# Attention and two MLPs on one core: the second and third weight blocks decoded through the staging buffer of the last attention pair

## The chip, the core and the metric

The kernel runs on one core of a Trainium2 chip. The core has a matrix engine (PE, with its weight loads shown as PEld), a vector engine (DVE), an activation engine (ACT), a general engine (POOL) and a queue engine (SP) that issues the transfers (DMA). Each engine works through its own queue strictly in order, so an instruction that waits holds up everything behind it on that engine. Engines wait for each other through semaphores. The metric is device time in microseconds of the whole program, one launch.

## The reference

```python
# q, k, v: (2, 8, 768, 64); centroids: (8, 16, 64)
q_assign, k_assign = argmax over 16 centroids of normalised q, k
mask = q_assign[:, :, :, None] == k_assign[:, :, None, :]
attn = softmax(where(mask, q @ k.T / 8, -1e9))
x = (attn @ v) as (1536, 512)            # token x (head, dim)
h = x @ w_in;   x = maximum(0.01 * h, h) @ w_out      # 512 -> 2048 -> 512
h = x @ w_in2;  out = (maximum(h, 0) ** 2) @ w_out2
```

All of it is float32. On the matrix engine each float32 factor is split into a high part and a low remainder, and a product is three matmuls (high·high, low·high, high·low).

## The kernel before

**Attention.** Heads are worked in 8 pairs of 6 units; a unit is 256 query rows of one head, and there are 48 (numbered 0 to 47, the last pair is 42 to 47). For each of a unit's two 128-row tiles PE makes the scores S (line 350), DVE takes the negated row maximum nm (373) and ACT the exponential e with its row sum r (383). ACT adds a small constant to r (394), DVE takes the reciprocal (397), POOL multiplies e by it (400). PE transposes e in three groups of four 128x128 blocks into T (413); of each, ACT writes the high part eh (424) and DVE the remainder el (430). PE multiplies both by V into A (448). There is one A buffer, so the next unit's A can start only when the two halves of this one are folded into xt, first by ACT (461), then by DVE (470). When a pair is done POOL splits xt into xh and xl (162 as `pool_copy`, 478); these are the first MLP's input.

**MLP.** The 1536 tokens are three blocks of 512, the hidden width 16 weight blocks of 128 for each MLP. A unit of the MLP is one weight block on one token block: 12 matmuls `h <- xh, xl x wh, wl` (725), t and g on ACT and DVE (738, 739), gh and gl (745, 746), and two units later 12 matmuls into o (767). The first token block needs no row of the last pairs, the other two need the last pair's xh and xl. There are four h buffers in PSUM and two of g.

**Weight blocks.** A block arrives as 1 MB of raw 64-bit numbers, wraw (121), and is decoded in six steps: load; mag on ACT (128, wt from wraw); shift, low and sign on DVE (132, 138, 145, all into wt); split, that is wh on ACT (156) and wl on POOL (157). Raw buffer and wt are single in each staging pool: a load waits until sign of the block before it has read wraw, and mag waits until wl of the block before it has read wt. `stg[0]` is opened at the last pair in memory that the pairs' preparation has left; `stg[1]` (`stgb`) is opened behind attention in memory that attention's tiles occupy, so its first load waits for the last transposes of the last unit. `EARLY` blocks are spread over the six units of the last pair; the others over the MLP's units by `plan`.

**Order.** PE, DVE, ACT and POOL follow an order written out by hand (`PLAN`) up to unit 42. From there a scheduler of the compiler sets the order on these engines, from its own estimate of times; so a change of what is decoded when changes the order of everything from the last pair on.

Of the kernel before, what the change touches and what calls it, by code (L numbers as in the profile page):

```python
# [8 lines left out]
F32 = mybir.dt.float32  # L9
F32R = mybir.dt.float32r  # L10
I32 = mybir.dt.int32
# [41 lines left out]
def attention_moe_moe_kernel(  # L53
# [14 lines left out]
    NT, DM = out.shape  # L68
# [3 lines left out]
    NU = NP * 2 * (KC // 2)  # L72
# [3 lines left out]
    NBLK = NT // N  # L76
    G = 4
    GROUPS = ([2, 2] + [G] * (NF // G - 1), [G] * (NF // G))
    EARLY = 2
    RING = 8  # L80
    WARM = (9,4,10)

# [29 lines left out]
    stg = []  # L112

    def decode_pieces(ci):

        m, f = divmod(ci, NF)
        st = {}

        def load():
            st["raw"] = stg[-1].tile([128, 2 * DM, 2], I32, tag="wraw", name="wraw")  # L120
            nc.sync.dma_start(
                out=st["raw"].rearrange("p a b -> p (a b)"), in_=(w1, w2)[m][f].bitcast(I32)
            )

        def mag():
            t = stg[-1].tile([128, 2 * DM], I32, tag="wt", name="wt")
            st["t"] = t
            nc.scalar.mul(out=t.bitcast(F32), in_=st["raw"][:, :, 1].bitcast(F32), mul=W_SHIFT)

        def shift():  # L130
            t = st["t"]
            nc.vector.tensor_scalar(
                out=t, in0=t, scalar1=3, scalar2=None, op0=ALU.logical_shift_left
            )

        def low():
            t = st["t"]
            nc.vector.scalar_tensor_tensor(  # L138
                out=t, in0=st["raw"][:, :, 0], scalar=29, in1=t,
                op0=ALU.logical_shift_right, op1=ALU.bitwise_or,  # L140
            )

        def sign():
            t = st["t"]
            nc.vector.scalar_tensor_tensor(
                out=t, in0=st["raw"][:, :, 1], scalar=-0x80000000, in1=t,
                op0=ALU.bitwise_and, op1=ALU.bitwise_or,
            )

        def split():  # L150
            t = st["t"].bitcast(F32)
            pool = next(q for q, n in ring if ci % RING < n)
            wh = pool.tile([128, 2 * DM], F32R, tag="wh", name="wh")
            wl = pool.tile([128, 2 * DM], F32R, tag="wl", name="wl")
            weights[m, f] = (wh, wl)
            nc.scalar.copy(out=wh, in_=t)  # L156
            nc.gpsimd.tensor_tensor(out=wl, in0=t, in1=wh.bitcast(F32), op=ALU.subtract)  # L157

        return [load, mag, shift, low, sign, split]

    def pool_copy(out, in_):
        nc.gpsimd.tensor_scalar(
            out=out, in0=in_, scalar1=1.0, scalar2=1.0, op0=ALU.mult, op1=ALU.mult
        )
# [175 lines left out]
    s_t, e_t, r_t, et_t, a_t, xt_t, n_t = {}, {}, {}, {}, {}, {}, {}  # L340
# [331 lines left out]
    }  # L672

    early = [f for i in range(EARLY) for f in decode_pieces(i)]
    for u in range(-1, NU + 5):
        if u == NU - UPP:
# [7 lines left out]
        for op in PLAN[FIRST[u] if p == 0 else u % UPP].split():  # L684
            if ":" in op:
                name, lag = op.split(":")
# [5 lines left out]
            else:  # L692
                name, ahead = op.split("@")
# [107 lines left out]
    for m in range(2):  # L801
        f = 0
        for g, size in enumerate(GROUPS[m]):
            for i in range(size):
                if ci >= EARLY:
                    pcs = decode_pieces(ci)
                    at = last + i * (began - last) // size
                    n = max((began - last) // size, 1)
                    for k, pc in enumerate(pcs):
                        plan.setdefault(at + k * n // len(pcs), []).append(pc)  # L810
                ci += 1
            last = began
            for b in range(NBLK):
                for i in range(size):
                    units.append((m, b, f + i, g, i == 0, i == size - 1))
            began = len(units)
            f += size
# [60 lines left out]
```

## Time and profile before

| | |
|---|---|
| device time, median of 3 runs | 793.46 us (792.37 to 793.86) |
| the profiled execution's own time | 790.98 us |
| its span, first to last instruction | 789.2 us |
| PE busy | 771.2 us, 98% of the span |
| DVE, ACT, POOL busy | 538.0, 412.7, 292.0 us |
| granted clock of PE | 1.000 (2.4 GHz) |

Attention fills the span up to about 266 us, the MLPs the rest. A row of the timeline is one instruction: start, duration, engine, line, what is written from what, and in brackets how long the engine stood idle before it and what released it. The durations of PE are modelled and overlap, so the distance of two starts tells what a matmul takes from the queue's time.

### The profile page before, as it was taken

The page shows a single profiled execution, that of the slowest core. Times are in us where ns is not written, and L with a number is a line of the kernel's source. Part 1 is how long each engine was busy: PE and PEld are TensorE (multiplying, and loading weights), DVE is VectorE, ACT ScalarE, POOL GpSimd, SP SyncE. Part 2 cuts the span into 40 slices and gives each one's busy share as a digit, 9 for nine tenths or more (in the row PEclk, how much of TensorE's full clock was granted, in tenths as well). Part 3 has the DMA queues.
Part 4 walks back from the last instruction along what each step waited for, and adds up shares of the span by engine and source line. Part 5 has one row for each costly group of instructions (what it writes and reads, how often), then busy time and mean ns, then how long its engine had stood idle before and what let it go on. Part 6 is the DMA issues. An engine that isn't in the chain of part 4 may idle for free.

```text
span 789.2 us, 11011 instructions
## 1 busy us (share of the span) xinstructions
PE 771.2 (98%) x4147; PEld 664.4 (84%) x4147; DVE 538.0 (68%) x772; ACT 412.7 (52%) x759; POOL 292.0 (37%) x257
## 2 busy tenths in 40 slices
PE   8999999999989999999999999999999999999998
PEld 8899999999977778888888888888888888888886
DVE  5899999999997378876665568387356547533333
ACT  6988988988996464443432344345344334222221
POOL 2989889888854322122220124352022012100000
PEclk9999999999999999999999999999999999999999
DMA  7584574564510323123221022013112103000102
GB/s 222 120 205 108 109 173 116 113 153 91 125 54 2 107 106 107 60 100 108 107 107 54 1 106 82 26 54 108 54 53 107 54 0 108 1 0 1 45 23 94
DMA packets 16005, 66.35 MB, mean 84 GB/s; under 512 B 2704, under 2 KB 2704, under 8 KB 10960
## 3 DMA queue, kind: packets, MB, share of 16 engines
q1 hardware_dynamic: 15952, 65.64, 28.7%
q8 instruction: 33, 0.54, 0.3%
q14 instruction: 20, 0.16, 0.1%
HBM read 44.60 MB, written 3.15 MB: 60 GB/s over the span
## 4 chain that ended last, share of the span: by engine, by line
PE 81%; DVE 11%; ACT 4%; DMA 1%; issue 1%; POOL 1%; SPq 0%; DVEq 0%; ACTq 0%
PE o L767 33%; PE h L725 33%; PE A L448 5%; PE T L413 5%; PE S L350 5%; DVE el L430 3%; DVE nm L373 3%; ACT e L383 2%; DVE xt L470 1%; ACT eh L424 1%; DVE ds L276 1%; PE ohT L305 1%; DVE m L275 1%; DMA rqk<-qk 1%; DVE wt L138 1%
## 5 line engine op out<-in xcount | busy, mean ns | idle before, releaser
L157 POOL TENSOR_TENSOR wl<-wt,wh 128x1024 fp32r<-128x1024 f32 x32 | 76.8, 2400 | 292.6 <-ACT wh L156 235.6
L725 PE MATMUL h<-xh,wh 128*128 128x512 f32 x384 | 150.6, 393 | 2.2 <-DVE g L739 2.2
L725 PE MATMUL h<-xh,wl 128*128 128x512 f32 x384 | 150.6, 392 | 0.0
L725 PE MATMUL h<-xl,wh 128*128 128x512 f32 x384 | 150.5, 392 | 0.0
L746 DVE TENSOR_TENSOR gl<-g,gh 128x512 fp32r<-128x512 f32 x96 | 95.4, 994 | 47.6 <-ACT gh L745 47.5
L430 DVE TENSOR_TENSOR el<-T,eh 128x512 fp32r<-128x512 f32 x144 | 94.8, 683 | 7.8 <-ACT eh L424 6.0
L745 ACT CAST gh<-g 128x512 fp32r<-128x512 f32 x96 | 59.6, 621 | 73.0 <-DVE g L742 42.7
L400 POOL TENSOR_SCALAR e<-e,r 128x768 f32<-128x768 f32 x96 | 88.0, 927 | 20.1 <-DVE r L397 14.7
L373 DVE TENSOR_REDUCE nm<-S 128x1 f32<-128x768 f32 x96 | 90.7, 946 | 4.6 <-PE S L254 2.2
L350 PE MATMUL S<-hb 128*128 128x384 f32 (+1 forms) x384 | 90.6, 350 | 3.0 <-ACT e L383 2.6
L383 ACT ACTIVATE e<-S,nm 128x768 f32<-128x768 f32 x96 | 87.0, 906 | 11.7 <-DVE nm L373 7.4
L742 DVE TENSOR_TENSOR g<-t 128x512 f32<-128x512 f32 x48 | 39.4, 822 | 72.8 <-ACT t L741 72.7
L725 PEld LDWEIGHTS h<-xh,wh 128*128 128x128 f32 x384 | 72.2, 188 | 18.5 <-DVE g L739 2.6
L741 ACT ACTIVATE t<-h 128x512 f32<-128x512 f32 x48 | 28.7, 598 | 112.0 <-PE h L725 111.9
L424 ACT CAST eh<-T 128x512 fp32r<-128x512 f32 x144 | 79.6, 585 | 12.9 <-PE T L413 12.3
L725 PEld LDWEIGHTS h<-xh,wl 128*128 128x128 f32 x384 | 72.2, 188 | 16.0
L725 PEld LDWEIGHTS h<-xl,wh 128*128 128x128 f32 x384 | 72.2, 188 | 15.9
L448 PE MATMUL A<-eh,vv 128*128 128x256 f32 x288 | 79.5, 306 | 3.5 <-DVE xt L470 3.5
L413 PE MATMUL T<-ident,e 128*128 128x128 f32 x576 | 81.0, 274 | 1.1 <-DVE el L430 1.0
L738 ACT ACTIVATE t<-h 128x512 f32<-128x512 f32 x48 | 28.6, 598 | 95.6 <-PE h L725 95.6
L767 PE MATMUL o<-gh,wl 128*128 128x512 f32 x192 | 75.3, 392 | 0.0
L767 PE MATMUL o<-gh,wh 128*128 128x512 f32 x192 | 74.5, 393 | 0.8 <-DVE xt L470 0.8
(105 smaller groups left out, 1454.0 us busy)
## 6 DMA issues: line engine op xcount, KB each, us to landing
wraw<-w SPq DMA_DIRECT2D x32, 1024.0 KB, 4.7
hb<-spl SPq DMA_DIRECT2D x14, 576.0 KB, 4.8
hb<-spl SPq DMA_DIRECT2D x42, 192.0 KB, 5.0
rqk<-qk SPq DMA_DIRECT2D x16, 384.0 KB, 4.5
rv<-v SPq DMA_DIRECT2D x8, 384.0 KB, 3.6
out<-ob SPq DMA_DIRECT2D x12, 256.0 KB, 2.1
twice<-qk SPq DMA_DIRECT2D x8, 192.0 KB, 6.4
hb<-st SPq DMA_DIRECT2D x28, 48.0 KB, 2.7
```

The source lines that it names most:

```text
L157: nc.gpsimd.tensor_tensor(out=wl, in0=t, in1=wh.bitcast(F32), op=ALU.subtract)
L350: nc.tensor.matmul(out=s[:, c, 0:HALF], lhsT=hb[0:k, a, i * 128 : (i + 1) * 128], rhs=hb[0:k, b, c * HALF : (c + 1) * HALF], start=(a == 0 ...
L373: nc.vector.tensor_reduce(out=n, in_=s_t[t][:, :, 0:HALF], axis=AX.XY, op=ALU.max, negate=True)
L383: nc.scalar.activation(out=e.rearrange("p (a b) -> p a b", a=2), in_=s_t.pop(t)[:, :, 0:HALF], func=AF.Exp, bias=n_t.pop(t), scale=1.0, ac ...
L400: nc.gpsimd.tensor_scalar(out=e_t[t], in0=e_t[t], scalar1=r_t[t // 2][:, t % 2 : t % 2 + 1], scalar2=1.0, op0=ALU.mult, op1=ALU.mult,)
L413: nc.tensor.transpose(T[:, o : o + 128], e_t[2 * u + b][:, kc * 128 : (kc + 1) * 128], ident)
L424: nc.scalar.copy(out=eh[:, 2 * g : 2 * g + 2, :].rearrange("p a b -> p (a b)"), in_=T_t[u, g])
L430: nc.vector.tensor_tensor(out=el[:, 2 * g : 2 * g + 2, :].rearrange("p a b -> p (a b)"), in0=T_t.pop((u, g)), in1=eh[:, 2 * g : 2 * g + 2, ...
L448: nc.tensor.matmul(out=A, lhsT=w, rhs=m[:, kc, :], start=(kc == 0 and i == 0), stop=(kc == KC - 1 and i == 1),)
L725: nc.tensor.matmul(out=h, lhsT=w[:, ws], rhs=x[:, kk, c], start=(kk == 0 and i == 0), stop=(kk == HP - 1 and i == 2),)
L746: nc.vector.tensor_tensor(out=gl, in0=g, in1=gh.bitcast(F32), op=ALU.subtract)
L767: nc.tensor.matmul(out=outs[o], lhsT=l, rhs=r, start=(first and i == 0), stop=(last and i == 2),)
```

## The change

Block 0 alone is now decoded during the last pair (`EARLY` 2 to 1). Blocks 1 and 2 are decoded through the same staging pool as block 0, `stg[0]`, in the code of the MLP; blocks 3 and later go through `stg[1]` as blocks 2 and later did. Ahead of block 1's load stands a copy of unit 45's reciprocal row sums (`r_t[NU - 3]`, 128x2 numbers) by POOL into the raw buffer, which the load then overwrites: so the load can't start before that copy.

```diff
--- before.py
+++ after.py
@@ -76,7 +76,7 @@
     NBLK = NT // N
     G = 4
     GROUPS = ([2, 2] + [G] * (NF // G - 1), [G] * (NF // G))
-    EARLY = 2
+    EARLY = 1
     RING = 8
     WARM = (9,4,10)
 
@@ -115,15 +115,18 @@
 
         m, f = divmod(ci, NF)
         st = {}
+        own = 0 if ci < 3 else -1
 
         def load():
-            st["raw"] = stg[-1].tile([128, 2 * DM, 2], I32, tag="wraw", name="wraw")
+            st["raw"] = stg[own].tile([128, 2 * DM, 2], I32, tag="wraw", name="wraw")
+            if ci == EARLY:
+                pool_copy(out=st["raw"][:, 0].bitcast(F32), in_=r_t[NU - 3])
             nc.sync.dma_start(
                 out=st["raw"].rearrange("p a b -> p (a b)"), in_=(w1, w2)[m][f].bitcast(I32)
             )
 
         def mag():
-            t = stg[-1].tile([128, 2 * DM], I32, tag="wt", name="wt")
+            t = stg[own].tile([128, 2 * DM], I32, tag="wt", name="wt")
             st["t"] = t
             nc.scalar.mul(out=t.bitcast(F32), in_=st["raw"][:, :, 1].bitcast(F32), mul=W_SHIFT)
```

Lines behind the edit are three higher in the changed kernel (the load's two are one and three higher). Since the scheduler orders all from unit 42 on, rows move on four engines; SP's are the same.

DVE, at the start of the moved stretch (the row maxima of unit 45), before:

```order
L373 TENSOR_REDUCE nm<-S 128x1 x2
L132 TENSOR_SCALAR wt<-wt 128x1024
L470 TENSOR_TENSOR xt<-A,xt 64x256
L397 RECIPROCAL r<-r 128x2
L430 TENSOR_TENSOR el<-T,eh 128x512
L138 SCALAR_TENSOR_TENSOR wt<-wraw,wt 128x1024
L430 TENSOR_TENSOR el<-T,eh 128x512
L373 TENSOR_REDUCE nm<-S 128x1
L430 TENSOR_TENSOR el<-T,eh 128x512
L145 SCALAR_TENSOR_TENSOR wt<-wraw,wt 128x1024
L397 RECIPROCAL r<-r 128x2
L470 TENSOR_TENSOR xt<-A,xt 64x256
```

and now:

```order
L376 TENSOR_REDUCE nm<-S 128x1
L473 TENSOR_TENSOR xt<-A,xt 64x256
L400 RECIPROCAL r<-r 128x2
L376 TENSOR_REDUCE nm<-S 128x1
L433 TENSOR_TENSOR el<-T,eh 128x512 x3
L376 TENSOR_REDUCE nm<-S 128x1
L473 TENSOR_TENSOR xt<-A,xt 64x256
L400 RECIPROCAL r<-r 128x2
L376 TENSOR_REDUCE nm<-S 128x1
```

The three decode steps of block 1 (L132, L138, L145) are gone from between the row maxima, folds and remainders.

DVE where the first MLP unit's g stands (L739 before, L742 now), beginning behind the last pair's row maxima, before:

```order
L470 TENSOR_TENSOR xt<-A,xt 64x256
L430 TENSOR_TENSOR el<-T,eh 128x512
L397 RECIPROCAL r<-r 128x2
L739 TENSOR_TENSOR g<-h,t 128x512
L746 TENSOR_TENSOR gl<-g,gh 128x512
L430 TENSOR_TENSOR el<-T,eh 128x512 x2
L470 TENSOR_TENSOR xt<-A,xt 64x256
L430 TENSOR_TENSOR el<-T,eh 128x512
L739 TENSOR_TENSOR g<-h,t 128x512
L746 TENSOR_TENSOR gl<-g,gh 128x512
```

and now:

```order
L400 RECIPROCAL r<-r 128x2
L135 TENSOR_SCALAR wt<-wt 128x1024
L433 TENSOR_TENSOR el<-T,eh 128x512
L141 SCALAR_TENSOR_TENSOR wt<-wraw,wt 128x1024
L742 TENSOR_TENSOR g<-h,t 128x512
L433 TENSOR_TENSOR el<-T,eh 128x512
L148 SCALAR_TENSOR_TENSOR wt<-wraw,wt 128x1024
L473 TENSOR_TENSOR xt<-A,xt 64x256
L433 TENSOR_TENSOR el<-T,eh 128x512
L749 TENSOR_TENSOR gl<-g,gh 128x512
L433 TENSOR_TENSOR el<-T,eh 128x512 x2
L473 TENSOR_TENSOR xt<-A,xt 64x256
```

Block 1's shift, low and sign (L135, L141, L148) now stand here, sign directly ahead of a fold (L473); before, this place had no decode step, but two MLP units' g and gl.

POOL, from unit 45's two multiplications by r to the split of the last pair's xt, before:

```order
L400 TENSOR_SCALAR e<-e,r 128x768 x2
L157 TENSOR_TENSOR wl<-wt,wh 128x1024
L400 TENSOR_SCALAR e<-e,r 128x768 x4
L162 TENSOR_SCALAR xh<-xt 128x768
L478 TENSOR_TENSOR xl<-xt,xh 128x768
L157 TENSOR_TENSOR wl<-wt,wh 128x1024 x18
```

and now:

```order
L403 TENSOR_SCALAR e<-e,r 128x768 x2
L165 TENSOR_SCALAR wraw<-r 128x2
L403 TENSOR_SCALAR e<-e,r 128x768 x4
L160 TENSOR_TENSOR wl<-wt,wh 128x1024
L165 TENSOR_SCALAR xh<-xt 128x768
L160 TENSOR_TENSOR wl<-wt,wh 128x1024
L481 TENSOR_TENSOR xl<-xt,xh 128x768
L160 TENSOR_TENSOR wl<-wt,wh 128x1024 x17
```

The new copy (L165 `wraw<-r`) stands right behind unit 45's multiplications; block 1's wl moved behind all of attention's, and block 2's wl came between xh and xl of the last pair.

On PE, 12 matmuls of the first MLP now stand ahead of the last pair's last transposes, where 36 stood; 22 more stand between these and the last A in both orders. From the end of the last A to the matmul into h that waits for block 2's unit (the first with block 2's wh) there are 38 matmuls of 128x512 before and 62 now.

## Rows read from the trace of the kernel before

**Rows 1.** The page, part 1: busy time, share and count of each engine.

```profile
PE 771.2 (98%) x4147; PEld 664.4 (84%) x4147; DVE 538.0 (68%) x772; ACT 412.7 (52%) x759; POOL 292.0 (37%) x257
```

**Rows 2.** Waits of PE, 215 to 300 us: total, times, longest.

```profile
PE h L725 <- DVE g L739: 2.2, 1, 2.2
PE A L448 <- DVE xt L470: 1.4, 1, 1.4
PE S L350 <- ACT e L383: 1.4, 1, 1.4
...
PE o L767 <- DVE xt L470: 0.8, 1, 0.8
```

**Rows 3.** Windows: PE, PEld, DVE, ACT, POOL busy (x), PEclk, DMA.

```profile
220.00:240.00 20.00, 15.86 (x109) 13.85 (x108) 19.66 (x29) 17.39 (x36) 12.80 (x10) 1.00 0.15 53
```

**Rows 4.** Timeline of DVE, 229 to 240 us: start, duration, instruction.

```profile
229.46 2.00 DVE L373 TENSOR_REDUCE nm<-S 128x1 f32<-128x768 f32 x2
...
232.75 0.69 DVE L430 TENSOR_TENSOR el<-T,eh 128x512 fp32r<-128x512 f32 x1
...
236.55 2.55 DVE L145 SCALAR_TENSOR_TENSOR wt<-wraw,wt 128x1024 int32<-128x1024 int32 x1
```

**Rows 5.** Timeline of ACT, 229 to 233 us.

```profile
229.34 1.16 ACT L128 ACTIVATE wt<-wraw 128x1024 f32<-128x1024 f32 x1
...
231.57 0.90 ACT L383 ACTIVATE e<-S,nm 128x768 f32<-128x768 f32 x1
```

**Rows 6.** Timeline of POOL, 232 to 242 us.

```profile
236.20 1.82 POOL L478 TENSOR_TENSOR xl<-xt,xh 128x768 fp32r<-128x768 f32 x1
239.35 1.79 POOL L400 TENSOR_SCALAR e<-e,r 128x768 f32<-128x768 f32 x2 [1.33 <-DVE r L397]
```

**Rows 7.** Chain of waits, 215 to 300 us: start, us, what.

```profile
227.72 1.44 PE A L448 x12
...
229.70 0.78 PE S L350 x4
...
245.66 4.41 PE h L725 x19
...
259.08 0.45 PE T L413 x4
...
259.59 4.66 DMA wraw<-w
...
264.33 1.15 ACT wt L128
...
265.51 0.71 DVE wt L132
...
266.24 1.22 DVE wt L138
...
267.49 0.44 DVE xt L470
...
268.01 1.87 POOL xh L162
...
269.95 1.85 POOL xl L478
271.80 2.37 POOL wl L157
...
274.19 1.14 ACT wt L128
...
277.34 0.70 DVE g L739
```

**Rows 8.** Instructions on wraw: ns least, median, most; starts.

```profile
L145 DVE SCALAR_TENSOR_TENSOR wt<-wraw,wt x32: 1202/1224/2553, 223.0 to 672.2; 128x1024 int32<-128x1024 int32 x32
```

**Rows 9.** POOL by line and form: busy us, mean ns.

```profile
L162 POOL TENSOR_SCALAR vv<-rv 128x768 fp32r<-128x768 f32 x7 | 5.8, 827 | 0.0
...
L100 POOL MEMSET mbi<- 32x1 f32 x1 | 0.1, 90 | 0.0
```

## The prediction

> **What bounds the kernel now.** I read the page's busy shares first: PE is busy 98% of the span, no other engine comes near [rows 1]. So time can only be won where PE stands still, and the next view is PE's waits. All the large ones fall in a stretch of some 50 us where attention hands over to the MLP; from 278 us to the end the view lists none. Behind the point where the order changes (230 us) there are four, 1.4 + 1.4 + 0.8 + 2.2 = 5.8 us [rows 2]. That is the most the change can win, by and large. Then I asked what ends each wait, with the windows, the timelines of DVE, ACT and POOL, and the chain.
>
> The first two belong together. Between 220 and 240 us DVE is busy 19.66 of 20 us [rows 3]: it, not PE, sets the pace there. Block 1's decode stands in the middle of attention's work. Its mag starts at 229.34 on ACT and pushes the exponential to 231.57 [rows 5], though the row maximum that it needs was ready at about 230.4 (the first of two from 229.46) [rows 4]: PE's wait for e. Its sign holds DVE for 2.55 us from 236.55 [rows 4], ahead of the fold that frees the A buffer: PE's wait for xt.
>
> The other two hang on block 2. Its load waits for the last transposes, 259.08 + 0.45, and lands 4.66 us after its issue; mag, shift and low follow, and low ends at 267.46, ahead of the last fold (267.49) [rows 7]. The last A ended at about 266 (259.5, 22 matmuls of 0.232 and one A of 1.44), so the fold is late by about a microsecond: the 0.8. From the fold a chain runs on: xh 1.87, xl 1.85, wl of block 2 2.37, mag of block 3 1.14 (it waits for wl, since wt is single), shift, low, then g at 277.34 [rows 7], which frees the h buffer PE waits for: the 2.2.
>
> **The change, part by part.**
>
> *Block 1 leaves the last pair.* DVE loses shift 0.71, low 1.22 and sign 2.55 (4.5 us) and ACT mag 1.16 and wh between 229 and 241 us. Both early waits lose their cause: -2.8 us. The work is not saved, it comes later; the question is what it holds up there.
>
> *It now stands behind the last row maxima.* Here I count both queues forward from 230 us to the A of unit 46, which waits for a fold standing right behind block 1's sign. DVE, from 229.46: 6 row maxima of 0.95, 12 remainders of 0.65 (0.69 alone [rows 4], less when they follow each other), 5 folds of 0.43, 4 short reciprocals (0.7 together), then shift 0.71, low 1.22, one g 0.70, sign 1.2 [rows 4, 7, 8]: 5.7 + 7.8 + 2.15 + 0.7 + 3.8 = 20.2, so it ends at 249.7. PE, from 230.5 (the S at 229.70 plus 0.78): 7 transposes 0.75, 4 A of 1.44, 4 S of 0.78, 12 groups of transposes of 0.44, 12 matmuls of 0.232 (4.41/19) [rows 7]: 0.75 + 5.8 + 3.1 + 5.3 + 2.8 = 17.7, so it would be there at 248.2. PE waits about 1.5 us; with a little for restarts I take 1.8. Bounds: 0.8, if remainders cost 0.60 and gaps are small; 4.3, if low and sign both take the 2.55 that a sign has cost beside POOL's xl [rows 6, 8] (1.8 + 1.35 + 1.3). I stay near the low end, since POOL's multiplications are done by then (about 245.8: last reciprocal at 243.9, 1.79 long) and its queue then waits for wh.
>
> *The copy and the load.* The trace has no copy of 128x2 on POOL; it lies between a memset's 0.09 and 0.83 for the same operation on 128x768 [rows 9], and I take 0.1, as it has two numbers a partition. It runs behind unit 45's multiplications (1.79 [rows 6]). By the DVE count their reciprocal comes 6.0 us after 229.46, at 235.5, so they end at about 237.3 and the load, 4.66 long, lands between 242.1 and 242.9. ACT reaches mag at about 243.4 (row maximum of the last tile at 241.5, e 0.90, then a fold, a cast and the row sums). So the hold costs nothing, with 0.5 to 1.3 us in hand. If that cover were gone, each microsecond would be one of PE's wait, because DVE is what bounds there. Queued behind mag on ACT are the casts of unit 46 and the first t; behind the copy on POOL the multiplications of units 46 and 47, which wait for later reciprocals; behind the load on SP only weight loads. Block 0's decode stays where it was.
>
> *Matmuls change sides.* 24 matmuls of the first MLP that filled PE ahead of the last transposes now stand behind the last A: 24 x 0.232 = 5.6 us. The last transposes come earlier by that, and by what is won ahead of them. The cover they gave attention's last units is the PE count above; it is not needed twice.
>
> *Block 2 through the old staging.* It need not wait for the last transposes, only for block 1's sign: its three DVE steps are over before the last fold. Block 3 takes its place in that race, but on DVE only its shift (0.71) can stand ahead of the fold, where shift and low did. I take the fold as ending 1.2 us after the last A (ACT's half, up to 0.35 behind shift, DVE's 0.44); before it was 2.0. The o that waits for it (0.8 before) now has 20 matmuls ahead of it behind that A, 4.6 us: hidden.
>
> *The chain behind the fold.* POOL now does wl of block 2 between xh and xl, so: xh 1.87, wl 2.37, xl 1.85, wl 2.37, mag 1.14, shift 0.71, low 1.22, g 0.70 = 12.2, with 0.4 for handing over and the 1.2 in front 13.8 us behind the last A. PE has 62 matmuls to do, 14.4 us. The same count for before: 2.0 + 9.9 + 0.4 = 12.3 against 38 matmuls and the 0.8, 9.6: a wait of 2.7, where 2.2 was measured. So the 2.2 falls away with 0.6 us to spare; I keep 0.2 for it. Bounds: 0, and 1.9 (below).
>
> *Sum.* -5.8 + 1.8 + 0.2 = -3.8 us, on the profiled execution 790.98 - 3.8 = 787.2. The three timed runs have a median of 793.46, 0.3% above it; the same step gives 789.7 us.
>
> **A rule weighed.** Sign took 2.55 us when xl had started 0.35 us before it, against 1.2 [rows 4, 6, 8]; xh took 1.87 us against 0.83 for the same form [rows 7, 9]. The Trainium skill, page "SBUF — State Buffer", section "SBUF: two separate sides", says that a DVE instruction with two SBUF inputs and a POOL instruction that reads SBUF share a port pair which the first to start holds for its whole length. The trace agrees. By that rule block 3's low and sign, which follow each other directly behind the last fold, could keep xh waiting twice: 2.4 + 0.83 in place of 1.87, and the sum would be -3.8 + 0.6 = -3.2 us. I go by the 1.87 of the row.
>
> **Rivals.**
>
> *All four waits go.* Steps of the decode fall into gaps of DVE that my count closes. For it: PE needs only 17.7 us where DVE needs 20.2, and ACT is not full. Against it: the DVE queue is fixed, and sign stands ahead of the fold. Time: 793.46 - 5.8 = 787.7.
>
> *The chain behind the last fold is late again.* Block 3's load is issued when the last transposes end, while block 2's may still run. If it lands one whole load after block 2's, it lands 2.3 us later than alone (issues 249.7 and 252.0 by my count), and block 3's mag stands ahead of the last fold on ACT: the fold comes 1.5 us later. With both port delays (about 1.2) the chain is 16.5 long against 14.4: a wait of 2.1 takes the old one's place. For it: that chain ended last before. Against it: 0.6 us in hand. Gain 5.8 - 1.8 - 2.1 = 1.9, time 791.6.
>
> *The waits form again elsewhere*, DVE's decode at 2.55 a step and the late chain together: 4.3 + 1.5 = 5.8, no change, 793.5.
>
> *Slower: the load of block 1 comes too late.* ACT then stands at mag with attention's last casts behind it, and the 24 matmuls that could have covered this are behind the last A. It breaks even when the load lands 3.8 us after ACT asks, at 247.2 by my count, and the kernel is slower by 0.2% from 248.8 on; landing at 250, it would be 793.46 + 2.8 = 796.3. For it: the hold makes the load wait for the sum of a late unit, and in the trace of before a load that started late was on the chain (4.66 us) [rows 7]. Against it: unit 45's multiplications began at 239.35 even with block 1's decode in the way [rows 6], which puts the landing at 246, before break-even.
>
> **Chances and range.** My forecast 0.56 (its own range 788.2 to 791.2), all waits gone 0.13, late chain 0.15, no change 0.07, slower 0.09. 0.2% is 1.6 us, about what a measurement can tell from no change. The late chain lies on that bound, so half of it counts as faster: 0.56 + 0.13 + 0.07 = 0.76 faster, 0.15 the same, 0.09 slower. The range goes from 787.2, all waits gone and restarts with them, to 793.2, where the late chain and half of the no-change case are inside: 0.13 or so is left out.
>
> **What would show it.** PE's waits: those for e and xt before 245 us gone; one or two for xt or el of 1 to 2 us together a little ahead of the first MLP units; the wait for g gone or under a microsecond. On ACT, mag of block 1 without idle time ahead of it. PE's first matmul with block 2's wh about 4 us earlier than 278.08. Wrong would be: a wait of ACT for `wraw` at block 1 above 1 us; PE's wait for g still near 2; or a sum of PE's waits behind 230 us above 4 us.

## The result and the profile after

| | before | after |
|---|---|---|
| median | 793.66 us (4 runs, 792.37 to 793.92) | 785.65 us (4 runs, 785.18 to 786.00) |
| profiled execution, its span | 790.98, 789.2 us | 785.70, 783.9 us |
| granted clock of PE in the profiled execution | 1.000 | 1.000 |

Ratio 0.9906 [0.9893, 0.9918]: 8.0 us or 0.9% faster, where 3.8 was forecast; 785.65 lies below the predicted range. The same two kernels timed again, on two different chips, gave 785.92 against 792.68 (0.9917 [0.9904, 0.9931]) and 786.02 against 792.41 (0.9914 [0.9901, 0.9928]). Between the two profiled executions lie 5.3 us. So there are two questions: where the 5.3 come from, and why the medians stand further apart than that.

PE's waits after, 215 to 300 us (who waits, for whom: us in total, times, longest); they answer to [rows 2]:

```profile
PE T L416 <- DVE el L433: 1.0, 1, 1.0
PE A L451 <- DVE xt L473: 0.9, 1, 0.9
PE h L728 <- DVE g L742: 0.4, 1, 0.4
PE A L451 <- DVE el L433: 0.3, 1, 0.3
PE T L416 <- POOL e L403: 0.2, 1, 0.2
```

The waits of 1.0 and 0.3 lie ahead of the moved stretch and stood in the profile before as well. Behind 230 us 0.9 + 0.4 + 0.2 = 1.5 us are left of 5.8: 4.3 us won. PE is still the bound. The window below answers to [rows 3]; it gives the length, then the busy time of PE, PEld, DVE, ACT and POOL with the count of instructions, the granted clock (1.00 is 2.4 GHz), and the share and GB/s of the DMA.

```profile
220.00:240.00 20.00, 18.69 (x139) 17.61 (x138) 19.75 (x34) 18.55 (x41) 13.84 (x13) 1.00 0.08 20
```

DVE is as full as it was (19.75 of 20), but now without block 1's three steps (block 0's sign lies in this window in both), so PE does 139 instructions there against 109. The rest of the 5.3, 1.0 us, is in no listed wait: by the distance of starts the same matmuls follow each other more closely up to the first one with block 2's wh, the scores by 0.6 us and the MLP's by 0.5. Where a matmul of the MLP is the first behind a wait or behind transposes, the next one starts 0.31 to 0.35 us later instead of 0.23; ahead of block 2's there were six such places and now there are two.

ACT, POOL, DVE and PE where block 1 is now decoded, timelines after (start, duration, instruction, idle time before it and its releaser), answering to [rows 4, 6]:

```profile
242.78 1.12 ACT L131 ACTIVATE wt<-wraw 128x1024 f32<-128x1024 f32 x1
```

```profile
237.17 0.20 POOL L165 TENSOR_SCALAR wraw<-r 128x2 f32<-128x2 f32 x1
...
243.95 3.29 POOL L403 TENSOR_SCALAR e<-e,r 128x768 f32<-128x768 f32 x2 [2.89 <-DVE r L400]
```

```profile
243.92 0.69 DVE L135 TENSOR_SCALAR wt<-wt 128x1024 int32<-128x1024 int32 x1 [0.44 <-ACT wt L131]
...
247.58 1.21 DVE L148 SCALAR_TENSOR_TENSOR wt<-wraw,wt 128x1024 int32<-128x1024 int32 x1
248.82 0.43 DVE L473 TENSOR_TENSOR xt<-A,xt 64x256 f32<-64x256 f32 x1
```

```profile
249.30 0.39 PE L451 MATMUL A<-eh,vv 128*128 128x256 f32 x1 [0.94 <-DVE xt L473]
```

The copy is cheap. Block 1's load is issued at 237.40 and lands 4.8 us later, at 242.2; ACT comes to mag at 242.78 and doesn't wait for it. The fold that frees A stands behind sign as the order showed, and PE's A starts at 249.30 after its 0.9 us. And the chain behind the last fold, answering to [rows 7]: DVE first, then POOL, then PE.

```profile
258.67 0.43 DVE L473 TENSOR_TENSOR xt<-A,xt 64x256 f32<-64x256 f32 x1
259.12 1.23 DVE L141 SCALAR_TENSOR_TENSOR wt<-wraw,wt 128x1024 int32<-128x1024 int32 x1
260.38 1.73 DVE L148 SCALAR_TENSOR_TENSOR wt<-wraw,wt 128x1024 int32<-128x1024 int32 x1
...
272.05 0.68 DVE L742 TENSOR_TENSOR g<-h,t 128x512 f32<-128x512 f32 x1
```

```profile
259.19 1.86 POOL L165 TENSOR_SCALAR xh<-xt 128x768 fp32r<-128x768 f32 x1 [6.35 <-DVE xt L473]
261.01 3.37 POOL L160 TENSOR_TENSOR wl<-wt,wh 128x1024 fp32r<-128x1024 f32 x1
264.34 2.29 POOL L481 TENSOR_TENSOR xl<-xt,xh 128x768 fp32r<-128x768 f32 x1
266.59 2.40 POOL L160 TENSOR_TENSOR wl<-wt,wh 128x1024 fp32r<-128x1024 f32 x1
```

```profile
272.79 0.50 PE L728 MATMUL h<-xh,wh 128*128 128x512 f32 x1 [0.41 <-DVE g L742]
```

From the last fold's end (259.1) to g's (272.7) it is 13.6 us; PE reaches the waiting h only 0.4 us before.

### The profile page after: what moved, and what is told of

Its sections match the earlier page's. It is cut to its first block, busy times and chain, and to the rows that moved or that the text cites. A ratio compares the mean times of both kernels' runs of the same rounds, so it can differ in the third digit from the quotient of the medians.

```text
span 783.9 us, 11017 instructions
## 1 busy us (share of the span) xinstructions
PE 770.7 (98%) x4147; PEld 665.6 (85%) x4147; DVE 535.4 (68%) x772; ACT 411.3 (52%) x759; POOL 294.0 (37%) x258
## 4 chain that ended last, share of the span: by engine, by line
PE 82%; DVE 11%; ACT 4%; POOL 1%; issue 1%; DMA 1%; DVEq 0%; ACTq 0%; POOLq 0%
PE o L770 33%; PE h L728 32%; PE A L451 5%; PE S L353 5%; PE T L416 5%; DVE el L433 4%; DVE nm L376 3%; ACT e L386 1%; DVE xt L473 1%; ACT eh L427 1%; DVE ds L279 1%; PE warm L202 1%; PE ohT L308 1%; DVE m L278 1%; DMA wraw<-w 1%
## 5 line engine op out<-in xcount | busy, mean ns | idle before, releaser
L770 PE MATMUL o<-gl,wh 128*128 128x512 f32 x192 | 75.3, 392 | 0.0
```

The source lines that it names most:

```text
L770: nc.tensor.matmul(out=outs[o], lhsT=l, rhs=r, start=(first and i == 0), stop=(last and i == 2),)
```

## The experiments

Each was timed beside the kernel before. "Waits" are PE's listed waits behind 230 us in the profiled execution. A ratio is that of the median to the median of before, with its 95% interval in brackets; "the clock" of an execution is the mean granted clock of the whole of it. e1 to e4, e5 to e8, e9 to e12 and e13 to e15 each ran together on one chip, with 792.86, 792.68, 792.81 and 792.41 us as the median of before.

### The clock

The profiled execution of before (790.98) was 2.7 us faster than its median. The profile of e2 (below) showed where such a difference can lie: behind the same wait of 2.2 us for g the granted clock fell. Windows of e2 (columns as above), then its PE, then two windows of before:

```profile
276.00:278.00 2.00, 0.90 (x4) 0.38 (x2) 1.63 (x2) 1.76 (x4) 0.00 (x0) 1.00 0.00 0
278.00:280.00 2.00, 0.94 (x3) 0.75 (x4) 1.97 (x4) 0.96 (x2) 0.00 (x0) 0.81 0.00 0
280.00:282.00 2.00, 2.00 (x6) 1.59 (x5) 2.00 (x4) 2.00 (x4) 0.00 (x0) 0.50 0.21 33
282.00:284.00 2.00, 2.00 (x9) 1.56 (x8) 1.91 (x3) 0.95 (x3) 1.82 (x1) 0.83 0.84 315
```

```profile
279.06 0.66 PE L726 MATMUL h<-xh,wh 128*128 128x512 f32 x1 [2.17 <-DVE g L740]
279.52 0.63 PE L726 MATMUL h<-xl,wh 128*128 128x512 f32 x1
279.94 0.63 PE L726 MATMUL h<-xh,wl 128*128 128x512 f32 x1
...
282.50 0.47 PE L726 MATMUL h<-xh,wl 128*128 128x512 f32 x1
282.81 0.39 PE L726 MATMUL h<-xh,wh 128*128 128x512 f32 x1
```

```profile
278.00:280.00 2.00, 1.92 (x8) 1.61 (x9) 2.00 (x4) 1.94 (x4) 0.00 (x0) 1.00 0.00 0
280.00:282.00 2.00, 2.00 (x10) 1.61 (x10) 2.00 (x4) 1.53 (x3) 0.80 (x1) 1.00 0.49 135
```

A clock of 0.50 is 1.2 GHz. From 279.52 to 282.50 seven matmuls stand 0.426 us apart instead of 0.232. The Trainium skill, page "TensorE: Matmul & The Clock Gate", section "Wait — 56ns, not 53.3ns?", gives 0.4267 us for 512 columns at the lower level; the trace agrees. In the profile of before the same wait of 2.18 us brought no fall (clock 1.00 in the windows behind it). There the first nine steps behind the wait take 2.20 us (278.08 to 280.28), in e2 3.75 (279.06 to 282.81): the fall costs 1.55 us, a little less than the 1.7 that the expectations below go by.

**e1, the kernel before once more.**

> The kernel before, unchanged, once more. Open: its profiled execution took 790.98 us, its four timed runs 792.4 to 793.9. Theory: its executions differ by up to 3 us from one to the next in some stretch that the change takes off the path (the port between DVE and POOL, or the load behind the last transposes), so this execution is anywhere from 791 to 794, and against the trace of before the difference lies between 220 and 280 us. Rival: the shown profile is from a chip on which everything is 0.3% faster; then this one takes 793 to 794 with the difference spread over the whole span, some 1.3 us of it by 400 us and the rest behind. Second rival: recording makes no difference of either kind and the same 790.98 comes out again.

792.96 us, 1.0009 [0.9999, 1.0019]: no difference. Over all 87 executions of the kernel before whose clock was listed, 13 have a mean clock of 1.000 and a median of 791.5 us, 72 have 0.998 or less and 792.9. The execution that I had read was one of the rarer kind; e1's profiled one, with a wait of 2.3 and clock 1.000, is another. The mean clock alone doesn't say where in the program it fell; e5 and e6 tie it to this wait.

**e5, PE kept busy in that wait** (kernel before, nine matmuls more; the edit is shortened here, its condition stands as a comment):

```diff
                 outs[o] = ps_o.tile([128, N], F32, tag="o", name="o")
+                # once, ahead of the h that waits for g
+                for _ in range(9): matmul(out=outs[0], lhsT=weights[0, 0][0][:, 0:128], rhs=xh[:, 0, 0:N])
```

> Kernel before, with nine more matmuls (128x512, into an o buffer that the real matmuls then overwrite) in PE's queue ahead of the h that waits 2.2 us for g. They take 9 x 0.232 = 2.1 us, so they fill the wait and win nothing by themselves. Theory (the wait brings the granted clock down to 1.2 GHz in most executions, which costs 1.7 us behind it): with PE busy there, mean clock 1.000 in all runs, median about 791.3, that is 1.5 to 2 us below the kernel before, although PE does more. Rival (the difference of 2.7 us between the profiled execution of before and its median has nothing to do with this wait): median within 0.5 us of before, clock still 0.997 to 0.999 in most runs.

Waits and PE of e5:

```profile
PE A L448 <- DVE xt L470: 1.5, 1, 1.5
PE S L350 <- ACT e L383: 1.4, 1, 1.4
PE T L413 <- DVE el L430: 1.0, 1, 1.0
PE o L767 <- DVE xt L470: 0.9, 1, 0.9
```

```profile
276.26 2.26 PE L755 MATMUL o<-xh,wh 128*128 128x512 f32 x9
278.60 0.50 PE L725 MATMUL h<-xh,wh 128*128 128x512 f32 x1
```

791.61 against 792.68, 0.9987 [0.9978, 0.9995]; clock 1.000 in six executions and 0.999 in five, where before has 0.998 or less in 19 of 21. PE does nine matmuls more and the program is 1.1 us faster: the fall belongs to this wait. The gain is smaller than the 1.5 to 2 us expected.

**e6, the wait put back into the changed kernel:** one DVE instruction more ahead of one g (shortened).

```diff
             nc.scalar.activation(out=t, in_=h, func=AF.Copy, scale=0.01)
+            if U == 2: nc.vector.tensor_tensor(out=t, in0=t, in1=t, op=ALU.max)
```

> Changed kernel, with one more DVE instruction (t = max(t, t)) ahead of the g that frees the h buffer; sign of block 3 slips ahead of g with it, so g comes about 1.7 us later and PE waits about 2.1 us there instead of 0.4. Theory (clock): 785.7 + 1.7 = 787.4 in executions whose clock holds, and about 789.0 where it falls behind the wait, which should be most of them: median 788.3 to 789.3, mean clock 0.997 to 0.999 in most runs. Rival (the wait costs its length alone): median 787.4, clock 1.000 in all.

```profile
274.00:276.00 2.00, 0.45 (x2) 0.41 (x3) 2.00 (x3) 1.16 (x3) 0.00 (x0) 1.00 0.15 25
276.00:278.00 2.00, 2.00 (x9) 1.58 (x8) 1.56 (x2) 2.00 (x4) 1.94 (x1) 0.76 0.89 270
278.00:280.00 2.00, 2.00 (x6) 1.55 (x5) 1.90 (x3) 0.17 (x1) 0.45 (x1) 0.50 0.55 229
```

PE waits 2.2 us for g and the clock falls behind it (windows above), in all five executions (0.997 to 0.998). 789.66 against 785.92 for **e8, the changed kernel again** on the same chip: 3.7 us for a wait that grew by 1.7 (0.5 in e8). The other 2.0 goes with the fall of the clock; 789.66 lies 0.4 above the expected range.

> Changed kernel once more, beside the others. Theory (clock): 785.7 within 0.4 us, mean clock 1.000 in all runs, and a spread under 1.5 us where before has one of 3 to 4.

All five executions of e8, and all 14 of the changed kernel, have clock 1.000; e8's own spread was 1.75 us.

### What the hold does

**e4, the changed kernel without the copy.**

```diff
-            if ci == EARLY:
-                pool_copy(out=st["raw"][:, 0].bitcast(F32), in_=r_t[NU - 3])
```

> The changed kernel without the copy that holds block 1's load back. Block 1's load may start behind sign of block 0, at about 224 us. Theory (the hold costs nothing and only sets what order the scheduler writes): if the order of DVE stays the same, the same time within 0.5 us; if the scheduler puts block 1's decode back between the row maxima, PE's waits for e and xt before 245 us come back and it is 2 to 4 us slower than the changed kernel. Rival (the copy and the late load cost something): faster than the changed kernel by 0.5 us or more.

794.0 us, 1.0014 [1.0004, 1.0023]. All four waits are back (2.2, 1.5, 1.4, 0.9), with a fifth of 0.4 for POOL's e, and e4 is some 8 us slower than the changed kernel, at least twice what was expected. DVE of e4:

```profile
229.18 2.00 DVE L374 TENSOR_REDUCE nm<-S 128x1 f32<-128x768 f32 x2
231.10 0.68 DVE L133 TENSOR_SCALAR wt<-wt 128x1024 int32<-128x1024 int32 x1
...
236.28 2.57 DVE L146 SCALAR_TENSOR_TENSOR wt<-wraw,wt 128x1024 int32<-128x1024 int32 x1
```

Without the copy nothing keeps the scheduler from putting block 1's decode where it was, between the row maxima. Here the copy acts through the order that the scheduler writes.

**e9, the hold alone** in the kernel before (EARLY 2, block 2 in the new pool), and **e14**, the same on another chip beside **e15**, the changed kernel a third time.

```diff
+            if ci == 1:
+                pool_copy(out=st["raw"][:, 0].bitcast(F32), in_=r_t[NU - 3])
```

> Kernel before (two early blocks, block 2 in the new pool), and one line more: block 1's load held by the row sums of unit 45. Theory (the hold is the whole change; pools and EARLY don't matter): 785 to 786.5, no wait of PE of 1.4 us or more behind 230 us, clock 1.000. Rival (block 2's early load through the old staging buffer is needed to take the chain behind the last fold off PE's path): the two early waits go but the wait for g of about 2 stays and with it the fall of the clock: 789.5 to 791.

> The hold alone once more, for comparison on one chip: 785.5 within 0.5. With a wait for g of 1.6 the clock stays at 1.000 behind it.

> The changed kernel once more, for comparison on one chip: 785.8 within 0.4, clock 1.000.

785.52 (0.9909 [0.9894, 0.9924]) and 785.92 (0.9916 [0.9903, 0.9930]); e15 786.02 (0.9914 [0.9901, 0.9928]). Two lines bring the whole gain. That no wait of 1.4 us or more would stay was wrong: e9 has 1.6 for g, e14 1.7. Waits of e14:

```profile
PE h L727 <- DVE g L741: 1.7, 1, 1.7
PE T L415 <- DVE el L432: 1.0, 1, 1.0
PE A L450 <- DVE el L432: 0.3, 1, 0.3
```

No wait for xt is left here, but 1.7 us for g: the sum (1.7) is near that of the changed kernel (1.5). Six of the eight executions have clock 1.000. Of the two others e14's (0.997) has no profile; in e9's profile (0.998) the fall has nothing to do with that wait: these windows at the program's start are the only ones below 1.00.

```profile
8.00:12.00 4.00, 4.00 (x29) 4.00 (x29) 1.68 (x4) 2.56 (x4) 0.00 (x0) 0.76 1.04 270
12.00:16.00 4.00, 3.64 (x26) 3.22 (x25) 3.01 (x4) 2.16 (x5) 0.95 (x1) 0.82 1.03 250
```

**e12, e11, e7: the hold by unit 44, 46 or 47.** `r_t[NU - 4]`, `r_t[NU - 2]` (this one with block 2 in the new pool), `r_t[NU - 1]`.

> Changed kernel, load of block 1 held by unit 44's sums: the copy comes at about 233.6 and the load lands at about 238.5, ahead of the last two row maxima. Theory (what counts is that the decode stands behind the row maxima): part of the decode slips back between them, one early wait of about 1 us returns, 786 to 787.5, clock 1.000. Rival (any hold is enough): 785.7.

> Changed kernel, load of block 1 held by unit 46's sums (copy at about 241.1 instead of 237.2, landing at about 246) and block 2 through the new pool. Theory: sign of block 1 then stands behind the fold for unit 46's A on DVE, so the 0.9 us wait for xt goes, and block 2 no longer waits for that sign: 784.5 to 785.5, the best version if the chain behind the last fold stays hidden. Rival: block 1 comes 4 us later, its wl falls beside xh or xl and the chain becomes late again by 1.5 to 2.5 with a fall of the clock: 787.5 to 790.

> Changed kernel, with block 1's load held by the row sums of unit 47 instead of unit 45; the copy comes 10 us later, behind unit 47's multiplications (about 247.3), so the load lands at about 252, and the scheduler puts block 1's decode behind all of attention's remainders. Theory (the hold only has to keep the decode behind the last row maxima; later than that it loses cover): both early waits stay gone and the new one before unit 46's A (0.9) goes too, but blocks 1 to 3 are then decoded one behind the other after 252, three times about 4.5 us, so that the first h with block 2 or 3 waits 2 to 4 us: 788 to 791. Rival (late-load price as in the prediction, each microsecond of landing one of PE's wait): landing 10 us later, mag asked for at 243.4 with 3.8 us of break-even, so clearly slower than before: 796 or more.

| held by | median | ratio | waits |
|---|---|---|---|
| unit 44 (e12) | 789.06 | 0.9957 [0.9945, 0.9969] | g 2.6, el 0.8 |
| unit 45 (e8) | 785.92 | 0.9917 [0.9904, 0.9931] | xt 0.9, g 0.5, e 0.2 |
| unit 46, new pool (e11) | 788.72 | 0.9958 [0.9944, 0.9972] | xt 3.3 |
| unit 47 (e7) | 791.00 | 0.9982 [0.9973, 0.9991] | g 2.8, others 1.7 |

The expectations of e11 and e12 missed. In e12 the early wait did not return; in its place the chain behind the last fold came late. In e11 block 1's low and sign each stand ahead of a fold that A waits for:

```profile
249.16 1.22 DVE L141 SCALAR_TENSOR_TENSOR wt<-wraw,wt 128x1024 int32<-128x1024 int32 x1
250.41 0.43 DVE L473 TENSOR_TENSOR xt<-A,xt 64x256 f32<-64x256 f32 x1
...
252.67 1.22 DVE L148 SCALAR_TENSOR_TENSOR wt<-wraw,wt 128x1024 int32<-128x1024 int32 x1
253.92 0.43 DVE L473 TENSOR_TENSOR xt<-A,xt 64x256 f32<-64x256 f32 x1
```

In all three PE waits 2.5 us or more at one place, and in their profiled executions (0.995 to 0.998) the clock falls behind that wait; e12's has a second fall, to 0.79, from 8 to 16 us. e11 differs from the changed kernel in block 2's pool as well, which by e3 (below) costs nothing under unit 45's hold. e7 also speaks on the price of a late load: the copy ended at 245.6, and the kernel was still faster than before, not 796.

**e10, EARLY 1 alone**, no hold and no old buffer: block 1's load waits for the last transposes.

> Kernel before with EARLY 1 alone: blocks 1, 2 and 3 all go through the new pool, whose first load waits for the last transposes (about 249.7). Theory: as where unit 47's sums held the load (load at 245.6 there, 791.0), but 4 us later, and block 2's load waits for block 1's sign: early waits of 1.4 + 1.4 gone, 4 to 6 us of waiting for block 2 in their place, and the clock falls behind it: 791 to 795. Rival (any late block 1 is as good as the hold): 785.5 to 787.

792.27, 0.9995 [0.9987, 1.0004]. The longest of PE's waits:

```profile
PE h L725 <- ACT wh L156: 5.0, 1, 5.0
```

This wh (259.81 to 260.85 on ACT) is the second of the program, so it is block 1's, and not block 2's as expected. The clock stays low for longer (mean 0.996). The early waits are gone here too (0.5 for xt at 250.99 and 0.2 for o are left), so taking block 1 away is not enough; it must come back in time.

### Block 2's staging

**e2, block 2 through the old buffer, without hold** (EARLY 2; the edit against before, shortened), and **e3, the changed kernel with block 2 in the new pool** (`ci < 2`).

```diff
+        own = 0 if ci < 3 else -1
-            st["raw"] = stg[-1].tile(...)
+            st["raw"] = stg[own].tile(...)
```

> Blocks 0 and 1 decoded in the last pair as before; block 2 alone goes through the old staging (no hold, EARLY stays 2). Theory, by the waits: the two early ones (1.4 and 1.4) stay, the two late ones (0.8 and 2.2) go or shrink, with some 0.5 of restarts: 2.5 to 3.5 us faster than before, about 790.5. Rival (the hand-over is bound by the early stretch alone): under 1 us faster.

> Block 1 out of the last pair and held, as in the changed kernel, but block 2 through the new pool behind the last transposes, as before. Theory: the early waits go (2.8 and 0.5 of restarts), and with 62 matmuls behind the last A in place of 38 the wait for g goes too even though block 2's low stands ahead of the last fold again: 4 to 7 us faster than before, within 1 us of the changed kernel. Rival (block 2's place in the old staging matters as much as block 1's move): 2.5 us or more behind the changed kernel.

e2: 793.47, 1.0007 [0.9998, 1.0017], waits as before (2.2, 1.4, 1.4, 0.8) and 0.4 for POOL's e, so the gain that was expected did not come. e3: 785.06, 0.9907 [0.9892, 0.9921]; waits xt 0.9 and e 0.2, none for g. Moving block 2 alone wins nothing, and leaving it out loses nothing.

**e13, hold alone plus the old buffer for block 2**, the candidate for the best version.

> Kernel before with the hold alone, and block 2 through the old staging buffer as well (two early blocks as before). Theory (time = 784.2 plus PE's listed waits behind 230 us, plus about 2 where the clock falls): the wait of 0.9 for xt is absent as with the hold alone, the wait of 1.6 for g as in the changed kernel under 0.5, so waits of at most 0.5: 784.2 to 785.0, below both the changed kernel and the hold alone by 0.6 to 1.2. Rival (the two trade against each other, since block 2's earlier decode holds up attention's folds): waits of about 1.5 again, 785.5 to 786.

787.51, 0.9942 [0.9929, 0.9954], slower than e14 and e15 beside it by 1.5 us. Waits of e13:

```profile
PE h L728 <- DVE g L742: 2.2, 1, 2.2
PE T L416 <- DVE el L433: 1.0, 1, 1.0
PE o L770 <- DVE xt L473: 0.6, 1, 0.6
```

The wait for g went up instead of down: block 3's decode now runs ahead of the last fold as block 2's did before, and the fold is late (263.81). No version was measurably faster than the changed kernel.

Put together: median less waits is about 784 with the hold by unit 45 where the clock held (785.9 - 1.5 = 784.4 after, 785.06 - 1.1 = 784.0 in e3, 785.92 - 1.7 = 784.2 in e14), and 784.7 (e13) to 787.6 (e4) where it fell in most executions (789.66 - 3.3 = 786.4 in e6, 791.0 - 4.5 = 786.5 in e7, 792.8 - 5.8 = 787.0 before). The clock is not all of that difference: before's executions with clock 1.000 give 791.5 - 5.8 = 785.7, some 1.3 us above after's, which is near the 1.0 in short gaps.

## Why the prediction was wrong

**The step that failed most is the last one: "the same step gives 789.7 us".** It carries a difference from one profiled execution over to the median as if the 0.3% between them had nothing to do with the change. But the profiled execution had clock 1.000, and most executions of before lose time behind the very wait that the change removes. The measured median, 785.65, lies 4.0 us below 789.7: 2.5 of these are that step (787.2 to 789.7), the other 1.5 are terms of the sum (787.2 against 785.70 in the traces). The range has the same flaw: its lower end, 787.2, is 793.46 less the listed waits and restarts, with nothing for the clock or for shorter gaps.

Executions with clock 1.000 on both sides are 791.5 - 785.9 = 5.6 us apart, near the 5.3 of the traces; the medians of all of them (792.8 and 785.9) 6.9. So 1.3 us of the gain is the clock; e5 gives 1.1 for it, e2's trace 1.55 and e6 2.0. The first comparison's 8.0 is 1.1 us more than 6.9: its before, 793.66, is 0.9 above the 792.8, and its after 0.2 below. The four lie among the other executions of before (790.6 to 794.6); their clock is not listed, and I have no cause for the 1.1.

**The sum, -5.8 + 1.8 + 0.2 = -3.8**, measured -5.3:

- *-5.8:* right in places and size. e4, where the decode goes back and all four return, and e9, where the hold alone takes three of them away and leaves 1.6 of the last, show it.
- *+1.8 ahead of unit 46's A:* right in place and cause, 0.9 in size. DVE was counted to 249.7 and was at 249.25 (fold 248.82 + 0.43); PE was counted to 248.2 and was there at 248.4 (249.30 - 0.94). POOL's multiplications were not done by 245.8: unit 47's two took 3.29 us beside DVE's steps instead of 1.79, and PE waited 0.2 for them, which the sum had at nothing.
- *+0.2 behind the last fold:* 0.4, near by luck. The count had 0.6 us in hand; the chain was 13.6 us long instead of 12.6, since POOL's four steps took 9.9 instead of 8.5 (wl 3.37 and xl 2.29, where 2.37 and 1.85 were counted).
- *Left out:* 1.0 us in short gaps between matmuls, the largest miss in the sum beside the 0.9 of the second term. I took PE's listed waits as all that can be won ("the most the change can win, by and large"), and they are not quite. This was read from traces and not tried by itself.

**Copy and load:** copy 0.20 (0.1 forecast), landing at 242.2 (242.1 to 242.9), mag at 242.78 without a wait. The hold cost nothing there. The signs that were named came out, two of them a little off in size: 0.9 us of waiting for xt instead of 1 to 2, and PE's first matmul with block 2's wh 5.3 us earlier (272.79) instead of about 4.

**Which part does it:** the prediction gave the early waits to block 1's leaving and the late ones to block 2's staging and the matmuls that change sides. e9 shows that the hold alone lowers the late chain's wait too (2.2 to 1.6) and removes the o wait; e2 and e13 show that block 2's staging has no worth of its own.

**The rule weighed:** the Trainium skill, page "SBUF — State Buffer", section "SBUF: two separate sides". I had low and sign keep xh waiting twice by it, 1.36 us more than the row. In the trace xh took 1.86, as the row that I went by, and sign and wl waited instead. The rule fits all three within 0.2 us: xh waits for low (259.12 to 260.35) and works 0.83; sign waits for xh's end at about 261.1 and works 1.2 (1.73 measured); wl, from 261.01, waits for sign's end at 262.1 and works 2.4 (3.37 measured). Here the turns alternate; neither engine gets two in a row. So the rule's extra time was nearer than the row (POOL's steps took 1.4 us more), but it fell on wl and xl and not on xh.

**Rivals:** *all four waits go* (787.7) was nearer in time, but by another cause, since 1.5 us of waits remain. *Late chain* and *no change* did not happen. *Load too late* did not happen either. In e7 the copy came 8.2 us later (245.38 against 237.17), so that the load landed at about 250.4, beyond the break-even of the working, and the kernel was 1.7 us faster than before. But the scheduler had put mag elsewhere (250.44, behind 0.39 us of waiting for the load), so the price with the order fixed was not tried.

## What to carry to other kernels

Before a sum made on one execution is put on a median, look at the clocks and times of all executions: a wait of PE has its own length as price and, where the clock falls behind it, a good part of that again (here 1.1 to 2.0 us for a wait of 2.2). Where a scheduler sets the order, a dependency that costs 0.2 us on an idle engine is a tool for moving work; try it alone before moving buffers, and on either side of the chosen unit, since one unit earlier or later cost 3 us here (later with block 2 in the new pool).

## What the runs showed of the hardware

- The same kernel, with a wait of 2.2 or 2.3 us in both of its profiles, had a mean clock of 0.998 or less in 72 of 87 executions and 1.000 in 13. The profiles show the clock fall within 1.5 us behind a wait of 2.2 us (e2, e6, e13), 2.5 (e11), 2.6 (e12) and 2.8 (e7), and within a wait of 5.0 (e10); behind 2.2 and 2.3 it also held (before, e1, e4), and behind 1.6 and 1.7 it held (e9, e14).
- In e9 and e12 it also fell once from 8 to 16 us, where PE was busy most of the time.
- Filling that wait with nine useless matmuls made the program 1.1 us faster.
- A copy of 128x2 numbers took POOL 0.20 us, more than twice a small memset's 0.09 [rows 9].
